# Attention rewritten for pairs of heads on two TensorE tiles

## The chip, the cores and the metric

The kernel runs on one core of one Trainium2 chip. A core has TensorE (PE; its weight loads are shown apart as PEld), VectorE (DVE), ScalarE (ACT), GpSimd (POOL) and the queues of SyncE (SP), all running on their own and meeting at semaphores. The metric is the device time of one execution in microseconds (us).

## The reference

Two stages follow one another. The attention has 4 batches of 8 heads, 768 positions of 64 numbers each. Keys are cut into 24 chunks of 32. For every query a bound per chunk is computed from the chunk's smallest and largest key; the six chunks with the highest bounds are kept, and the softmax runs over their keys up to the query's own position.

```
ub = sum(max(q * k_min, q * k_max))          # per query and chunk
top_chunks = argsort(where(causal, ub, -1e9))[-6:]
scores = q @ k.T / 8;  mask = (chunk in top_chunks) & (key <= query)
attn = softmax(where(mask, scores, -1e9));  out = attn @ v
```

The second stage is a mixture of experts over the 3072 rows of 512 numbers: each row goes to the expert with the highest gate logit (8 experts), each expert keeps its 80 rows with the highest gate weight, computes `gate * (relu(x @ w1) @ w2)`, and all other rows are zero.

## The kernel before

The attention phase runs through 32 heads one by one (L381 to L388), everything in float32. Per head:

- `prologue1` loads q, k and v and transposes q and k with TensorE (L267, L269), twelve transposes of 128 rows by 64 columns into psA and psB.
- `prologue2` copies them into `srhs` and `slhs` (ACT), makes the positive and negative part of q (`qstk`) and the chunk maxima and minima (`kstk`) on DVE, multiplies both (L282), takes the six best of 24 with six `max` instructions (L287), transposes the 0/1 selection (L292) and writes it, scaled to 0 or -80000, into rows 64 to 87 of `srhs` (L294). Rows 64 to 87 of `slhs` hold a fixed table of which key lies in which chunk. So the mask is part of the score matmul, which has 64 + 24 = 88 rows.
- `do_scores` computes the scores with keys on partitions, for each block of 128 keys only the queries from its own block on (L306; 768, 640, 512, 384, 256 and 128 columns). ACT takes the exponential (L311), DVE multiplies the diagonal block by a triangle (L314).
- `do_av` multiplies 21 blocks of the exponentials (as weights) by v with a column of ones (L323), so that column 64 of the result is the softmax sum; the queries lie on the output's partitions.
- `do_norm` divides on DVE and writes the rows in float32 and bf16 (L333 to L339). After a batch's last head it transposes the rows (L345), multiplies by the gate weights (L353) and computes gate weight and expert of each row (L360 to L375).

The second phase, behind a barrier (L390), sorts out the 80 rows per expert on DVE (L430 to L454), gathers them by a matmul with a 0/1 matrix (L480, L484), runs the experts (L497, L510), and scatters back in 24 turns: eight bf16 transposes (L516), a copy (L519), eight matmuls (L521), a copy and a store.

The order on each engine is the order in which the code issues. A helper class notes who wrote and read each buffer last and puts semaphore waits in front of an instruction. In the kernel before, an instruction also waits for an earlier one of its own engine when both write the same buffer, unless both are marked as accumulating; the transposes L267, L269, L292, L345 and L516 are not marked. There is one buffer of most kinds, so heads overlap only where the loop is written so: the transposes of the next head come before L323 of this one, and `prologue2` of the next head behind it.

Of the kernel before, what the change touches and what calls it, by code (L numbers as in the profile page):

```python
# [4 lines left out]
ALU = mybir.AluOpType  # L5
# [3 lines left out]
I32 = mybir.dt.int32  # L9
AX = mybir.AxisListType.X  # L10

NEGSEL = -1.0e9
BIGM = 8.0e4
CHUNK = 32
TOPK = 6
NCANDP = 16


class _Sync:
# [3 lines left out]
    def __init__(self, nc):  # L23
        self.nc = nc
        self.engines = {
            "pe": nc.tensor, "act": nc.scalar, "dve": nc.vector, "gp": nc.gpsimd,
            "sp": nc.sync, "acd": nc.scalar, "gpd": nc.gpsimd,
        }
        self.dma_engines = {"sp", "acd", "gpd"}
        self._cms = {}  # L30
        self.sems = {}
        self.cnt = {}
        self.last_write = {}
        self.last_reads = {}
        self.waited = {}
        for key in self.COMPUTE:
            self._mk(key)

    def _mk(self, key):
        cm = self.nc.semaphore("sy_" + key)  # L40
        self._cms[key] = cm
        self.sems[key] = cm.__enter__()
        self.cnt[key] = 0

    def sem(self, key):
        if key not in self.sems:
            self._mk(key)
        return self.sems[key]
# [5 lines left out]
    def _wait(self, waiter, semkey, val):  # L54
        if val <= 0:
            return
        wk = (waiter, semkey)
        if self.waited.get(wk, 0) >= val:
            return
        self.waited[wk] = val  # L60
        self.engines[waiter].wait_ge(self.sems[semkey], val)

    def op(self, ekey, fn, reads=(), writes=(), dsem=None, accum=False):
        is_dma = ekey in self.dma_engines
        semkey = dsem if dsem is not None else ekey
        inc = 16 if is_dma else 1
        for r in reads:
            w = self.last_write.get(r)
            if w is not None and not (accum and w[0] == semkey and w[2]):
                self._wait(ekey, w[0], w[1])  # L70
        for wres in writes:
            w = self.last_write.get(wres)
            if w is not None and not (accum and w[0] == semkey and w[2]):
                self._wait(ekey, w[0], w[1])
            for sk, sv in self.last_reads.get(wres, {}).items():
                self._wait(ekey, sk, sv)
        inst = fn()
        if semkey not in self.sems:
            self.sem(semkey)
        newval = self.cnt[semkey] + inc  # L80
        inst.then_inc(self.sems[semkey], inc)
        self.cnt[semkey] = newval
        for wres in writes:
            self.last_write[wres] = (semkey, newval, accum)
            self.last_reads[wres] = {}
        for r in reads:
            d = self.last_reads.setdefault(r, {})
            d[semkey] = max(d.get(semkey, 0), newval)
        return inst

    def wait_final(self, waiter, semkey):
        self._wait(waiter, semkey, self.cnt[semkey])

    def barrier_all(self):
        for wtr in self.COMPUTE:
            for prod in self.COMPUTE:
                if prod != wtr:
                    self._wait(wtr, prod, self.cnt[prod])


def bass_quest_chunk_select__then__topk_capacity_drop_kernel(
# [15 lines left out]
    NQT = S // 128  # L117
    NCH = S // CHUNK
    TOKT = B * NQT
    DB = Dm // 128  # L120
    FB = Fd // 128
    LROWS = D + NCH
    SCALE = 1.0 / float(D) ** 0.5
    EC = E * CAP
    assert S % 128 == 0 and D == 64 and Dm == H * D and CAP % 8 == 0 and E == 8
# [3 lines left out]

    with ExitStack() as pers, ExitStack() as phA, ExitStack() as phB:  # L130

        _alcnt = [0]

        def al(stack, shape, dt=F32, psum=False, nm=None):
            _alcnt[0] += 1
            name = (nm or "t") + "_" + str(_alcnt[0])
            if psum:
                return stack.enter_context(nc.psum_tensor(name, list(shape), dt))
            return stack.enter_context(nc.sbuf_tensor(name, list(shape), dt))

        x_bf = al(pers, [128, TOKT, Dm], BF16, nm="x_bf")
        gate_sb = al(pers, [128, TOKT], nm="gate_sb")
        eidx_sb = al(pers, [128, TOKT], nm="eidx_sb")
        ident_f = al(pers, [128, 128], nm="ident_f")
        ident_bf = al(pers, [128, 128], BF16, nm="ident_bf")
        caus_c = al(pers, [128, NQT, NCH], nm="caus_c")
        cbias_c = al(pers, [128, NQT, NCH], nm="cbias_c")
        ctri_c = al(pers, [128, 128], nm="ctri_c")
        esel_c = al(pers, [128, E, E], nm="esel_c")
        bmask_c = al(pers, [8, E, CAP], nm="bmask_c")  # L150
        wg_sb = al(pers, [128, DB, E], nm="wg_sb")
        ones8 = al(pers, [8, 128], nm="ones8")

        NSLOT = 4
        w1slot = [al(pers, [128, DB, Fd], BF16, nm="w1slot") for _ in range(NSLOT)]
        w2slot = [al(pers, [128, FB, Dm], BF16, nm="w2slot") for _ in range(NSLOT)]


        sy = _Sync(nc)

        with nc.Block() as blk:

            @blk.sync
            def _body(_unused):
# [5 lines left out]

                tmp_i = al(phA, [128, 1024], I32, nm="tmp_i")
                psA = al(phA, [128, 768], F32, True, nm="psA")
                psB = al(phA, [128, 768], F32, True, nm="psB")
# [389 lines left out]
```

## Time and profile before

| | us |
|---|---|
| runs of the kernel before | 1590.32, 1596.66, 1603.84 (median 1596.66) |
| span of the profiled execution | 1590.3 |
| its own time | the span; the fastest run shown, 1590.32, is the same within 0.1 |
| attention phase in the profile | 0 to 1112 |
| expert phase | 1112 to 1590 |
| TensorE busy | 1180.6 (74%) |
| VectorE busy | 604.3 (38%) |

The page shows the engines' busy time, then the chain that ended last, then groups of instructions by line. A group's row gives the tile written, the tiles read, the weights' shape (partitions * columns) and the moving operand's shape. A float32 matmul stands in the trace as two matmul records with a weight load each (L323 is 21 matmuls a head, 672 in all, and has 1344 records); a transpose and a bf16 matmul stand as one.

### The profile page before, as it was taken

Reading aid. Unit: us, or ns where it says so; the run is one execution under the profiler, and the core shown is the slowest. Engines: PE = TensorE matmul, PEld = TensorE weight load, DVE = VectorE, ACT = ScalarE, POOL = GpSimd, SP = SyncE. Lnnn points to the kernel's source line nnn. Section 1 sums busy time; section 2 is a strip of 40 time slices with the busy share of each in tenths; the row PEclk is TensorE's granted clock in tenths of the full one; section 3 lists DMA queues with packets and bytes.
Section 4 is the critical chain, followed back from the end, with each engine's and each line's share of the span. In section 5 each row is a group of like instructions: output and inputs, shape, how many; then the busy total and the mean of one; then the engine's idle time right before and its main releaser. Section 6 shows DMA issues by size and latency. Waiting matters only on the chain.

```text
span 1590.3 us, 11275 instructions
## 1 busy us (share of the span) xinstructions
PE 1180.6 (74%) x4100; PEld 691.1 (43%) x4100; DVE 604.3 (38%) x1812; ACT 193.6 (12%) x337; POOL 15.2 (1%) x26
## 2 busy tenths in 40 slices
PE   6888886888888678988967898885661004778887
PEld 3556554555655445645644565553110002433332
DVE  4343342344343243343314333432338995111010
ACT  1111111112112112112101111111000000010000
POOL 2000000000000000000000000000000000100000
PEclk9555555555555555555555555555785556875555
DMA  9401000001000000100100010000000000660101
GB/s 191 86 15 30 15 15 15 15 15 30 15 15 20 10 15 21 25 15 21 25 1 15 20 25 15 5 6 0 0 0 0 0 0 0 111 114 34 40 33 40
DMA packets 91846, 42.68 MB, mean 27 GB/s; under 512 B 76432, under 2 KB 84624, under 8 KB 91792
## 3 DMA queue, kind: packets, MB, share of 16 engines
q0 software_dynamic: 12544, 16.78, 6.1%
q1 hardware_dynamic: 54160, 18.90, 4.8%
q10 hardware_dynamic: 25088, 6.29, 1.8%
q8 instruction: 33, 0.54, 0.1%
q14 instruction: 21, 0.17, 0.0%
HBM read 52.45 MB, written 6.29 MB: 37 GB/s over the span
## 4 chain that ended last, share of the span: by engine, by line
PE 73%; DVE 21%; issue 3%; ACT 2%; DMA 1%; SPq 0%; DVEq 0%; POOL 0%; ACTq 0%; POOLq 0%
PE psE L323 16%; PE psA L306 11%; PE psB L306 8%; PE psX L521 5%; PE psB L292 5%; PE psC L282 4%; PE psT L516 4%; PE psG L435 3%; PE psB L269 3%; PE psA L345 3%; PE psA L267 3%; PE psC L353 3%; DVE top_37 L287 2%; DVE I_64 L446 2%; DVE V_63 L445 2%
## 5 line engine op out<-in xcount | busy, mean ns | idle before, releaser
L323 PE MATMUL psE<-v_ext,e_sb 128*128 128x65 f32 x1344 | 260.2, 384 | 0.0
L323 PEld LDWEIGHTS psE<-v_ext,e_sb 128*128 128x128 f32 x1344 | 259.1, 302 | 0.0
L306 PE MATMUL psA<-srhs,slhs 88*128 88x512 f32 (+1 forms) x256 | 201.1, 889 | 44.4 <-DVE srhs L294 30.2
L306 PE MATMUL psB<-srhs,slhs 88*128 88x128 f32 (+2 forms) x256 | 158.9, 724 | 1.8
L292 PE MATMUL psB<-ident_f,sel 128*24 128x128 f32 x192 | 74.5, 388 | 86.6 <-DVE sel L290 77.2
L311 ACT ACTIVATE e_sb<-psA 128x768 f32<-128x768 f32 (+2 forms) x96 | 57.3, 596 | 573.6 <-PE psA L306 573.6
L306 PEld LDWEIGHTS psA<-srhs,slhs 88*128 88x128 f32 x256 | 69.6, 317 | 125.0 <-PE psA L306 52.1
L306 PEld LDWEIGHTS psB<-srhs,slhs 88*128 88x128 f32 x256 | 73.9, 319 | 108.7 <-PE psB L306 52.2
L314 DVE TENSOR_TENSOR e_sb<-e_sb,ctri_c 128x128 f32<-128x128 f32 x192 | 55.9, 291 | 141.8 <-ACT e_sb L311 141.7
L521 PE MATMUL psX<-Ybf,selTj 80*128 80x512 bf16 x192 | 86.2, 630 | 18.8 <-DVE selTj L519 18.8
L285 DVE TENSOR_TENSOR ubm<-psC,cbias_c 128x144 f32<-128x144 f32 x32 | 9.9, 308 | 201.7 <-PE psC L282 201.7
L435 PE MATMUL psG<-rhsX,esel_c 128*8 128x512 f32 x96 | 55.5, 741 | 39.5 <-DVE rhsX L430 24.6
L267 PE MATMUL psA<-ident_f,q_nat 128*64 128x128 f32 x192 | 80.0, 417 | 4.4 <-DMA q_nat<-in_q_dram 4.4
L269 PE MATMUL psB<-ident_f,k_nat 128*64 128x128 f32 x192 | 80.0, 417 | 3.1 <-DMA k_nat<-in_k_dram 0.5
L462 PE MATMUL psG<-bd_67,ones_12 8*128 8x512 f32 (+1 forms) x4 | 2.5, 776 | 104.6 <-DVE bd_67 L456 104.6
L282 PE MATMUL psC<-kstk,qstk 128*128 128x24 f32 x384 | 76.5, 355 | 4.5 <-DVE kstk L279 4.5
L292 PEld LDWEIGHTS psB<-ident_f,sel 128*24 128x24 f32 x192 | 18.2, 95 | 137.2 <-DVE sel L290 80.9
L282 PEld LDWEIGHTS psC<-kstk,qstk 128*128 128x128 f32 x384 | 75.6, 298 | 4.8 <-DVE kstk L279 4.8
L345 PE MATMUL psA<-ident_f,x_f_46 128*128 128x128 f32 x96 | 45.3, 472 | 38.8 <-DVE x_f_46 L336 22.3
L519 DVE COPY selTj<-psT 80x1024 bf16<-80x1024 bf16 x24 | 16.5, 686 | 151.1 <-PE psT L516 151.1
L516 PE MATMUL psT<-ident_bf,sel_all 128*80 128x128 bf16 x192 | 62.1, 324 | 9.7
L294 DVE TENSOR_SCALAR srhs<-psB 24x768 f32<-24x768 f32 x32 | 30.4, 949 | 86.9 <-PE psB L292 86.9
(93 smaller groups left out, 1008.8 us busy)
## 6 DMA issues: line engine op xcount, KB each, us to landing
w1slot<-in_moe_w_dram POOLq DMA_DIRECT2D x8, 1024.0 KB, 18.0
w2slot<-in_moe_w_dram POOLq DMA_DIRECT2D x8, 1024.0 KB, 18.5
q_nat<-in_q_dram SPq DMA_DIRECT2D x32, 192.0 KB, 2.8
k_nat<-in_k_dram SPq DMA_DIRECT2D x32, 192.0 KB, 3.1
v_ext<-in_v_dram ACTq DMA_DIRECT2D x32, 192.0 KB, 2.6
out_dram<-otile SPq DMA_DIRECT2D x24, 256.0 KB, 2.0
wg_sb<-in_moe_w_gate_dram SPq DMA_DIRECT2D x1, 16.0 KB, 1.9
```

What stands on the lines that cost most here:

```text
L267: sy.op("pe", lambda qt=qt, buf=buf: pe.transpose(psA[0:D, ts(qt)], q_nat[buf][:, qt, :], ident_f[:]), reads=[f"qnat{buf}", "ident_f"], wr ...
L269: sy.op("pe", lambda qt=qt, buf=buf: pe.transpose(psB[0:D, ts(qt)], k_nat[buf][:, qt, :], ident_f[:]), reads=[f"knat{buf}", "ident_f"], wr ...
L282: sy.op("pe", lambda o_ap=o_ap, qt=qt: pe.matmul(o_ap, qstk[:, ts(qt)], kstk[:], start=True, stop=True), reads=["qstk", "kstk"], writes=[" ...
L292: sy.op("pe", lambda qt=qt: pe.transpose(psB[0:NCH, ts(qt)], sel[:, qt, :], ident_f[:]), reads=["sel", "ident_f"], writes=["psB"])
L306: sy.op("pe", lambda sps=sps, c0=c0, c1=c1, lhsK=lhsK, kt=kt: pe.matmul(sps[:, c0:c1], lhsK, srhs[:, 128 * kt + c0:128 * kt + c1], start=T ...
L311: sy.op("act", lambda sps=sps, kt=kt, ncol=ncol: ac.activation(e_sb[kt][:, 0:ncol], sps[:, 0:ncol], ACTF.Exp, scale=SCALE), reads=[pskey], ...
L314: sy.op("dve", lambda kt=kt: ve.tensor_tensor(e_sb[kt][:, 0:128], e_sb[kt][:, 0:128], ctri_c[:], ALU.mult), reads=[ekey, "ctri_c"], writes ...
L323: sy.op("pe", lambda lhsA=lhsA, kt=kt, qb=qb, buf=buf: pe.matmul(o_of(qb), lhsA, v_ext[buf][:, kt, :], start=(kt == 0), stop=(kt == qb)), ...
L345: sy.op("pe", lambda bd=bd, qt=qt: pe.transpose(psA[:, ts(qt)], x_f32[:, qt, bd * 128:(bd + 1) * 128], ident_f[:]), reads=["x_f32", "ident ...
L435: sy.op("pe", lambda e=e, c0=c0, c1=c1, rx=rx: pe.matmul(psG[0:8, c0:c1], esel_c[:, e, :], rx[:, c0:c1], start=(e == 0), stop=(e == E - 1) ...
L516: sy.op("pe", lambda j=j, e=e: pe.transpose(psT[0:CAP, ts(e)], sel_all[:, j, e * CAP:(e + 1) * CAP], ident_bf[:]), reads=["sel_all", "iden ...
L521: sy.op("pe", lambda e=e: pe.matmul(psX[:, 0:Dm], selTj[:, ts(e)], Ybf[:, e, :], start=(e == 0), stop=(e == E - 1)), reads=["selTj", "Ybf" ...
```

## The change

The attention is written anew for pairs of heads (16 pairs), and the helper class too. The expert phase's instructions are the same. In parts:

- Two heads lie side by side on partitions: head 0 on 0 to 63, head 1 on 64 to 127. One 128 by 128 transpose (L354) serves both.
- The bounds use one block-diagonal table for both heads and two accumulating matmuls per block of queries (L375, L377), `q * k_min + relu(q) * (k_max - k_min)`; the first block of 128 queries is left out, since it has no more than four chunks.
- The scores (L405) have 64 rows, and the two heads alternate between the upper and the lower half of TensorE's rows, with outputs in two PSUM banks. The mask is a separate bf16 matmul of 64 rows per head added to them (L411): -65536 for chunks that are not selected, transposed in bf16 (L392).
- The exponential of both heads is one ACT instruction of up to 1024 columns (L416). The triangle is set on GpSimd by `affine_select` (L420). GpSimd also adds up the exponentials over key blocks (L436).
- The values (L447) have v as weights (64 columns), so that the two heads lie on the output's lower and upper partitions, each with half of TensorE's columns. The softmax sums come from matmuls with one column of ones (L458). One matmul per block of 128 queries (L469) turns the result back into rows and gives the gate logits as well; DVE divides (L476, L480). `gate` works on 6 blocks at once.
- The loop is pipelined over pairs: bounds of pair i+1 stand between scores and values of pair i, transposes of pair i+2 behind the values. q, k and v are loaded three pairs ahead. The weights of the first four experts are loaded one half each behind the first eight pairs.
- The new helper class makes TensorE wait for no write or read of its own, and other engines only for their own writes; waits that another wait implies are left out.

```diff
-                for gidx in range(NG):
-                    do_scores(gidx)
-                    if gidx + 1 < NG:
-                        prologue1(gidx + 1)
-                    do_av(gidx)
-                    if gidx + 1 < NG:
-                        prologue2(gidx + 1)
-                    do_norm(gidx)
...
+        for res in r:
+            for sk, val in self.lw.get(res, {}).items():
+                want((sk, val), ekey == "pe")
+        for res in w:
+            for sk, val in self.lw.get(res, {}).items():
+                want((sk, val), ekey == "pe")
+            for sk, val in self.lr.get(res, {}).items():
+                want((sk, val), not is_dma)
...
+    STEPS = [
+        [(0, 0, 512, 0)],
+        [(1, 128, 640, 0)],
+        [(2, 256, 768, 0)],
+        [(0, 512, 768, 0), (4, 512, 768, 256)],
+        [(3, 384, 768, 0), (1, 640, 768, 384)],
+        [(5, 640, 768, 0)],
+    ]
...
+                    for st, pieces in enumerate(STEPS):
+                        s = st % 2
+                        for pi, (kt, q0, q1, c) in enumerate(pieces):
+                            for h in range(2):
+                                pr = slice(h * 64, h * 64 + 64)
+                                o = SC[s][:, h * 512 + c:h * 512 + c + q1 - q0]
+                                op("pe", lambda: pe.matmul(o, kT[j][pr, ts(kt)], qT[j][pr, q0:q1], start=True, stop=False),
...
+                            for h in range(2):
...
+                                op("pe", lambda: pe.matmul(o, ind[pr, ts(kt)], unsT[j][pr, b0 - 128:q1 - 128],
...
+                        op("act", lambda: ac.activation(Ex[st][:], src, ACTF.Exp, scale=SCALE),
...
+                        op("gp", lambda: gp.affine_select(a, a, pattern=[[0, 2], [1, 128]], compare_op=ALU.is_ge, fill=0.0,
...
+                            op("gp", lambda: gp.tensor_tensor(o, in0, in1, ALU.add),
...
+                            for h in range(2):
...
+                                op("pe", lambda: pe.matmul(OB[pr, q0:q1], vn[s][:, kt, h, :], Ex[st][:, h, c:c + q1 - q0],
...
+                            a = Ex[0][:, h, 0:128] if t == 0 else ES[:, h, ts(t)]
+                            op("pe", lambda: pe.matmul(o, a, one1[:], start=True, stop=True),
...
+                            op("pe", lambda: pe.matmul(OB[:, bk * 512 + m * XW:bk * 512 + (m + 1) * XW], oT[:, ts(t)], xr[:, p, :],
...
+                for i in range(NP):
+                    scores(i)
+                    if i + 1 < NP:
+                        bounds(i + 1)
+                    values(i)
+                    if i + 3 < NP:
+                        load(i + 3)
+                    if i + 1 < NP:
+                        unselT(i + 1)
+                    if i + 2 < NP:
+                        transposes(i + 2)
+                    if i < 2 * NSLOT:
+                        wload(i // 2, i % 2)
+                    sums(i)
+                    rows(i)
+                    if i % NPB == NPB - 1:
+                        gate(i // NPB)
```

TensorE, before, one head (the transposes of the next head stand ahead of the values L323; L306 are the scores):

```order
L267 MATMUL psA<-ident_f,q_nat 64x128
L269 MATMUL psB<-ident_f,k_nat 64x128
L323 MATMUL psE<-v_ext,e_sb 128x65 x21
L282 MATMUL psC<-kstk,qstk 128x24 x6
L292 MATMUL psB<-ident_f,sel 24x128 x6
L306 MATMUL psA<-srhs,slhs 128x512
L306 MATMUL psA<-srhs,slhs 128x256
```

Between the values L323 and the next scores L306 stand the bounds and the mask of the very head whose scores follow.

TensorE, in the change, one pair from its third score step on (L405 scores, L411 mask, L375 and L377 bounds of the next pair, L447 values, L392 and L354 transposes for later pairs, L458 sums, L469 rows; `x2` are the two heads):

```order
L405 MATMUL SC_17<-qT,kT 128x512 x2
L411 MATMUL SC_17<-unsT,ind 128x512 x2
...
L375 MATMUL M_20<-kbd,qT 128x48
L377 MATMUL M_20<-kbd,rq 128x48
...
L447 MATMUL OB<-Ex,vn 64x512 x2
L447 MATMUL OB<-Ex,vn 64x384 x2
...
L392 MATMUL MB<-ident_bf,uns 128x128 x5
L354 MATMUL SC_17<-ident_f,qn 128x128 x6
L354 MATMUL SC_18<-ident_f,kn 128x128 x6
L458 MATMUL M_20<-one_63,Ex 128x1 x2
L458 MATMUL M_20<-one_63,ES 128x1 x10
L469 MATMUL OB<-xr,oT 128x144 x6
```

Every heavy float32 matmul now stands next to one of the other head, and between scores and values, where the head before had the chain L282 to L294, the bounds of another pair stand.

GpSimd, in the change, one pair but for its last addition (Ex are the exponentials, ES their sums; sy_act and sy_gp are semaphores of ScalarE and of GpSimd itself):

```order
L420 AFFINE_SELECT Ex<-Ex 128x2x128 [waits sy_act] x2
L436 TENSOR_TENSOR ES<-Ex 128x2x384 [waits sy_gp]
L420 AFFINE_SELECT Ex<-Ex 128x2x128 [waits sy_act]
L436 TENSOR_TENSOR ES<-ES,Ex 128x2x256 [waits sy_gp]
L420 AFFINE_SELECT Ex<-Ex 128x2x128 [waits sy_act]
L436 TENSOR_TENSOR ES<-Ex 128x2x256 [waits sy_gp]
L436 TENSOR_TENSOR ES<-ES,Ex 128x2x128 [waits sy_gp]
L436 TENSOR_TENSOR ES<-ES,Ex 128x2x256 [waits sy_gp]
L420 AFFINE_SELECT Ex<-Ex 128x2x128 [waits sy_act]
L436 TENSOR_TENSOR ES<-ES,Ex 128x2x128 [waits sy_gp]
L436 TENSOR_TENSOR ES<-ES,Ex 128x2x384 [waits sy_gp]
L420 AFFINE_SELECT Ex<-Ex 128x256 [waits sy_act]
```

Before, GpSimd had no instruction between the heads; now six selects and eight additions per pair stand in one queue, and the values on TensorE read what the selects write.

## Rows read from the trace of the kernel before

**Rows 1.** The page: its first line, the engines' busy time, the chain by engine.

```profile
span 1590.3 us, 11275 instructions
PE 1180.6 (74%) x4100; PEld 691.1 (43%) x4100; DVE 604.3 (38%) x1812; ACT 193.6 (12%) x337; POOL 15.2 (1%) x26
...
PE 73%; DVE 21%; issue 3%; ACT 2%; DMA 1%; SPq 0%; DVEq 0%; POOL 0%; ACTq 0%; POOLq 0%
```

**Rows 2.** Windows: stretch, its length, busy by engine, granted TensorE clock, DMA.

```profile
0.00:1112.00 1112.00, 914.62 (x3104) 592.97 (x3104) 417.88 (x1647) 172.28 (x297) 8.45 (x17) 0.54 0.12 25
...
1197.00:1302.00 105.00, 0.44 (x1) 0.44 (x2) 103.33 (x55) 0.00 (x0) 0.00 (x0) 0.51 0.00 0
...
1415.00:1590.00 175.00, 143.75 (x386) 52.72 (x384) 17.15 (x25) 14.33 (x24) 0.00 (x0) 0.51 0.10 36
```

**Rows 3.** Timeline of TensorE, one head: start, length, line, operands, count, [idle before].

```profile
631.90 0.39 PE L267 MATMUL psA<-ident_f,q_nat 128*64 128x128 f32 x1
...
634.97 9.08 PE L323 MATMUL psE<-v_ext,e_sb 128*128 128x65 f32 x42
643.84 2.70 PE L282 MATMUL psC<-kstk,qstk 128*128 128x24 f32 x12
648.95 2.62 PE L292 MATMUL psB<-ident_f,sel 128*24 128x128 f32 x6 [2.41 <-DVE sel L290]
652.61 3.35 PE L306 MATMUL psA<-srhs,slhs 88*128 88x512 f32 x4 [1.04 <-DVE srhs L294]
...
660.03 1.49 PE L306 MATMUL psB<-srhs,slhs 88*128 88x384 f32 x2
661.30 1.06 PE L306 MATMUL psA<-srhs,slhs 88*128 88x256 f32 x2
...
662.93 0.39 PE L267 MATMUL psA<-ident_f,q_nat 128*64 128x128 f32 x1
```

**Rows 4.** Groups by line and shape: busy time, mean ns, idle before.

```profile
L484 PE MATMUL psG<-sel_all,x_bf 128*128 128x128 bf16 x96 | 21.8, 227 | 0.0
```

**Rows 5.** Windows inside single stages, columns as in the second group.

```profile
622.00:632.00 10.00, 9.88 (x17) 4.07 (x16) 5.27 (x27) 3.03 (x6) 0.00 (x0) 0.50 0.00 1
635.00:643.80 8.80, 8.80 (x43) 8.80 (x43) 3.00 (x4) 1.44 (x2) 0.00 (x0) 0.50 0.21 47
1117.00:1121.00 4.00, 4.00 (x6) 0.58 (x5) 0.18 (x1) 0.00 (x0) 0.00 (x0) 0.50 0.00 0
1122.00:1124.00 2.00, 2.00 (x6) 0.36 (x4) 0.00 (x0) 0.00 (x0) 0.00 (x0) 1.00 0.00 0
...
579.00:583.00 4.00, 4.00 (x38) 4.00 (x38) 2.88 (x4) 0.55 (x1) 0.00 (x0) 1.00 0.44 100
```

**Rows 6.** Groups by line and shape, ScalarE.

```profile
L311 ACT ACTIVATE e_sb<-psA 128x768 f32<-128x768 f32 x32 | 25.9, 809 | 528.1 <-PE psA L306 528.1
...
L311 ACT ACTIVATE e_sb<-psB 128x128 f32<-128x128 f32 x32 | 8.9, 277 | 6.5 <-PE psB L306 6.5
```

**Rows 7.** Groups by line, GpSimd.

```profile
L235 POOL IOTA tmp_i<- 88x768 int32 x1 | 0.8, 764 | 0.6 <-DVE v_ext L232 0.6
L191 POOL IOTA tmp_i<- 128x144 int32 x1 | 0.3, 262 | 0.5 <-DVE ident_bf L188 0.5
```

**Rows 8.** Timeline of TensorE, one turn of the last loop.

```profile
1421.63 3.02 PE L516 MATMUL psT<-ident_bf,sel_all 128*80 128x128 bf16 x8
1425.43 3.60 PE L521 MATMUL psX<-Ybf,selTj 80*128 80x512 bf16 x8 [0.78 <-DVE selTj L519]
1428.82 0.31 PE L516 MATMUL psT<-ident_bf,sel_all 128*80 128x128 bf16 x1
```

**Rows 9.** Timeline, the end of the attention phase.

```profile
1070.28 0.16 DVE L333 TENSOR_SCALAR rec<-psE 128x1 f32<-128x1 f32 x1 [8.26 <-PE psE L323]
...
1111.91 0.15 DVE L375 CAST eidx_sb<-idx_52 128x1 f32<-128x1 uint32 x1
```

**Rows 10.** Timeline of TensorE, the first scores of the run.

```profile
21.43 3.36 PE L306 MATMUL psA<-srhs,slhs 88*128 88x512 f32 x4 [1.04 <-DVE srhs L294]
```

More of the change, by code (lines that the diff above doesn't have):

```diff
@@ L91, in wait_final, with _learn @@
-    def wait_final(self, waiter, semkey):
-        self._wait(waiter, semkey, self.cnt[semkey])
+    def _learn(self, clock, ev):
+        sk, val = ev
+        if clock.get(sk, 0) < val:
+            clock[sk] = val
+        best = None
+        for v, snap in reversed(self.snaps[sk]):
+            if v <= val:
+                best = snap
+                break
+        if best:
+            for k2, v2 in best.items():
+                if clock.get(k2, 0) < v2:
+                    clock[k2] = v2
@@ L94, in barrier_all, with _implied, wait_for @@
+    def _implied(self, a, b):
+        c = {}
+        self._learn(c, a)
+        return c.get(b[0], 0) >= b[1]
+    def wait_for(self, waiter, keys):
+        for k in keys:
+            if self.cnt.get(k, 0):
+                self.queue[waiter].wait_ge(self.sems[k], self.cnt[k])
+                self._learn(self.clock.setdefault(self.stream.get(waiter, waiter), {}), (k, self.cnt[k]))
     def barrier_all(self):
@@ new lines, in _body @@
+                load(0)
+                v128 = iv(128, [1, 128])
+                op("gp", lambda: gp.iota(v128, pattern=[[-1, 128]], base=0, channel_multiplier=1), w=["ti"])
+                op("dve", lambda: ve.tensor_scalar(ident_f[:], v128, 0, None, ALU.is_equal), r=["ti"], w=["ident_f"])
+                for j in range(2):
+                    op("dve", lambda: ve.memset(kbd[j][:], 0.0), w=KBD[j])
+                op("dve", lambda: ve.memset(uns[:], 0.0), w=["uns"])
+                op("dve", lambda: ve.memset(one1[:], 1.0), w=["one1"])
@@ new lines, in _body @@
+                transposes(0)
+                bounds(0)
+                unselT(0)
+                transposes(1)
+                for i in range(NP):
[15 more added lines that the diff above has]
+                        gate(i // NPB)
@@ L390, in _body @@
                 sy.barrier_all()
+                XB = [f"x_bf{i}{bk}" for i in range(NP) for bk in range(2)]
+                XS = [f"xb{j}" for j in range(TOKT)]
+                EI = [f"eidx{b}" for b in range(B)]
+                GS = [f"gate{b}" for b in range(B)]
                 phA.close()
-                psG = al(phB, [128, TOKT * 128], F32, True, nm="psG")
-                psX = al(phB, [128, 512], F32, True, nm="psX")
-                psT = al(phB, [128, 1024], BF16, True, nm="psT")
```

736 lines of the change are left out of this document (387 added, 349 removed), and 3 rows, old and new, of the table AVS.

## Prediction

> **What bounds the kernel now.** I read the page first: TensorE is busy for 74% of the span and for 73% of the chain [rows 1]. The windows by stage then split the span [rows 2]: attention ends at 1112.0, the experts take the other 478.3 (1590.3 - 1112.0), 105 of them on DVE alone. The timeline of one head [rows 3] shows where attention's time lies: from transpose to transpose a head takes 31.0 us (631.90 to 662.93), of which TensorE waits 2.41 and 1.04 for DVE and otherwise works. [...]
>
> **Unit prices, at 0.50.** A float32 matmul is two records. L306 with 384 columns takes 661.30 - 660.03 = 1.27 us [rows 3], 3.31 ns per column. L323 has only 65 columns, yet 42 records take 643.84 - 634.97 = 8.87 [rows 3], 0.42 us per matmul; its weight loads fill the same stretch, as the third number of that window says [rows 5], so 0.42 us is what a float32 matmul with 128 weight columns costs however narrow it is. At clock 1.00, 38 records in 4 us [rows 5] make it 0.21. A transposed float32 block costs (634.97 - 631.90) / 12 = 0.26. [...]
>
> **The change, per pair of heads.** What TensorE issues, at 0.50:
> - 12 transposes x 0.26, taken as before although they load 128 columns instead of 64 and no longer wait on each other: 3.1.
> - Bounds, 10 matmuls x 0.42: 4.2. Mask transposes, 5 x 128 bf16 columns: 0.5.
> - Scores: 2688 columns per head, 8.9 us, and 2560 mask columns, 2.1; for two heads 22.0 one after the other, 11.0 if the halves of the array work fully side by side.
> - Values: 2688 columns per head, 8.9; 17.8 or 8.9.
> - Sums, 12 x 0.42: 5.0. Rows, 6 x 144 columns: 2.9.
>
> No row here has two matmuls in different halves of the array, so the overlap is the first unknown, between none and full. I take overlap, but by the order in which matmuls come: TensorE takes them in program order [rows 3], so head 1's first record can start only once head 0's second has started. With N the time of one bf16 pass, a piece is 2N alone, 2N shared by the heads, then head 1's second record beside head 0's mask (2N): 6N against 5N full and 10N serial. Scores then cost 13.4; values, without a mask, reach 4N per pair of matmuls, 8.9. Sum: 3.1 + 4.2 + 0.5 + 13.4 + 8.9 + 5.0 + 2.9 = 38.0 at 0.50 and 19.0 at 1.00, against 62 for two heads before.
>
> [...]
>
> **The clock** is the second unknown. L306, 88 rows, stays at 0.50 through 10 us without a gap; L323 stays there too in this head; L435, 128 rows and 512 columns, is at 0.50 for its first 4 us and at 1.00 afterwards; L323 holds 1.00 in a head that enters it so [rows 5]. In the change rows, scores and values use all 128 rows, if the halves overlap, and follow each other with only the bounds between; the sums, one column wide, are the weak place. So I take 4 us at 0.50 from the start of the rows stage (2.9 of rows, 1.1 of scores), the other 12.3 of scores at 1.00 as 6.2, bounds 2.1, values 4.5, transposes 1.8, and for the sums 3.8, midway between 2.5 and 5.0.
>
> **GpSimd** is the third. Its only compute rows are index patterns: (764 - 262) ns over 768 - 144 elements is 0.80 ns per element plus 0.15 us [rows 7]. A pair has six selects of 256 elements and eight additions of 3840 in all. Bounds: 0.80 throughout gives 6.4 us per pair (5376 x 0.80 + 14 x 0.15), three streams for two reads and a write, 2.4, gives 15. I take 2.4 for additions and 0.8 for selects, 12.5, since an addition moves three times the data of a pattern. [...] At 12.5 GpSimd stays below TensorE's time, but its queue is serial: the last select stands behind seven additions. An exponential of 1024 columns costs 1.02 us (809 ns at 768 and 277 ns at 128 [rows 6], so 0.83 per column), so from the first exponential to the last select some 14 us pass, and values that could start at 9 us and end at 14 end at about 17: a stall of 3. Behind each of the first eight pairs GpSimd also issues one weight load; TensorE reads it only in the expert phase, so I cost it at nothing.
>
> A pair: 4 + 6.2 + 2.1 + 4.5 + 3 + 1.8 + 3.8 = 25.4, with 0.6 for seven changes of stage 26. ACT has 5.5 us of exponentials and 3.3 of copies by the same line, DVE 25 instructions at its mean of 0.33 us (604.3 / 1812 [rows 1]), 8.3; both lie beside TensorE's work, and without that cover either would bound a pair at under 10.
>
> **Around the pairs.** The first scores start at 21.4 now [rows 10]; more loads, constants and the bounds of a whole pair make it 25. The last pair has no bounds and transposes, -5. The end of attention takes 41.6 now (1070.3 to 1111.9 [rows 9]), since the last head's division, four rounds of transposes and copies, the gate matmuls and six chains of small instructions follow one another; afterwards the division of the last pair and one such chain remain, some 13 instructions x 0.33 = 4. Attention: 25 + 16 x 26 - 5 + 4 = 440.
>
> **Experts.** A turn of the last loop takes 1428.82 - 1421.63 = 7.19; eight transposes and the copy take 3.80 of it (1421.63 to 1425.43), since each waits for the one before it [rows 8]. Unchained they stream at 0.11 each: 8 x 0.11 + 0.22 + 0.80 for the copy = 1.90. That is 1.9 x 24 = 46 saved, with the clock left at 0.51 [rows 2]. Multiplying the rows by their gate loses its chain too, 2. 478.3 - 48 = 430.
>
> **Sum:** 440 + 430 = 870. The profiled execution is the span, 1590.3, and the median of the runs is 0.4% above it, which I neglect.
>
> **Rivals.**
> - *The clock does not rise in the scores.* For: L306 never got it. Against: it had 88 rows. Values then begin at 0.50 (4 + 2.5): 2.9 + 13.4 + 4.2 + 6.5 + 1.8 + 3.8 + 0.6 = 33.2, 985 in all; never anywhere, 39 a pair, 1078. Chance 0.27.
> - *The halves do not overlap.* For: nothing here shows overlap in float32. Against: rows and PSUM banks are disjoint. Scores 22.0 at 0.50, values 4 + 6.9: 46 a pair, about 1190; 30 a pair if all of it ran at 1.00 (930), 56 if none (1350). Chance 0.17.
> - *Slower than before: GpSimd becomes the bound.* Its queue is serial and feeds the values. Against: it decides only from (1590.3 - 430 - 24) / 16 = 71 us per pair, which means 10 us per select instead of 0.35, or additions five times my upper bound. Price then 1600 and more. For: no select has a row. Chance 0.02.
> - *The change does not do what it says* would leave 1112 + 430 = 1542: only if every pair still took two heads' time. Chance 0.01.
>
> My forecast, with the pair at 21 (fast GpSimd, all at 1.00) to 29, is 780 to 920 and has 0.53. The range to 1150 takes in the slow clock and the mildest part of serial halves; it starts at 770.
>
> **Numbers.** 870, 770 to 1150. One per cent either way, 16 us, is what this kernel's runs can tell. Only the GpSimd rival is slower; a result within 1% needs the sum to be off by 700 us. Faster 0.96, same 0.01, slower 0.03.
>
> **What would show it.** Right: for each piece of L405 the second head's records start while the first head's run; the granted clock of attention above 0.75; TensorE idle before the last L447 matmuls, released by GpSimd L420; L516's eight transposes in about 1.1 us. [...]

## The result and the profile after

The changed kernel takes 761.7 us (median; 759.5 to 796.7 in four runs) against 1597.7 for the kernel before: a ratio of 0.476 [0.473, 0.479]. That is faster, as forecast, and 8 us below the low end of the range. Ratios compare the executions within 1.5% of each kernel's fastest, while medians and ranges take all. The rows are from another execution of the changed kernel, with a span of 760.3; the longest took 796.7, and nearly all of the difference between the two lies in the last loop (below).

The page: span, busy time, granted clock in 40 slices.

```profile
span 760.3 us, 8659 instructions
PE 511.2 (67%) x3632; PEld 312.4 (41%) x3636; DVE 318.3 (42%) x619; ACT 159.4 (21%) x221; POOL 209.9 (28%) x254
...
PEclk9999999999999999999868887555555699969999
```

Windows: attention and the last loop (answering to [rows 2]).

```profile
0.00:382.00 382.00, 338.95 (x2640) 238.08 (x2640) 134.58 (x453) 138.12 (x181) 203.18 (x245) 0.95 0.40 73
...
682.00:758.00 76.00, 55.86 (x376) 29.91 (x376) 15.81 (x23) 14.33 (x24) 0.00 (x0) 1.00 0.21 80
```

Attention ends at 382 where it was 1112, with TensorE's clock at 0.95 where it was 0.54. The last loop takes some 76 us at 1.00 where 175 were at 0.51. In the clock row the nines up to the middle are attention, the low stretch behind them the sorting, and the end the last loop. From the end of attention to the last loop it is 298 us (382 to 680), 303 before (1112 to 1415).

One pair on TensorE (answering to the head of [rows 3]):

```profile
178.89 1.13 PE L405 MATMUL SC<-qT,kT 64*128 64x512 f32 x4
...
180.02 1.02 PE L405 MATMUL SC<-qT,kT 64*128 64x512 f32 x4
...
185.43 0.42 PE L375 MATMUL M<-kbd,qT 128*128 128x48 f32 x2
...
187.79 2.15 PE L447 MATMUL OB<-Ex,vn 128*64 128x512 f32 x12
190.86 2.60 PE L447 MATMUL OB<-Ex,vn 128*64 128x128 f32 x28 [0.91 <-POOL Ex L420]
193.91 0.44 PE L447 MATMUL OB<-Ex,vn 128*64 128x128 f32 x4 [0.46 <-POOL Ex L420]
194.29 0.45 PE L392 MATMUL MB<-ident_bf,uns 128*128 128x128 bf16 x5
...
195.89 0.50 PE L458 MATMUL M<-one,Ex 128*128 128x1 f32 x4
...
198.49 1.90 PE L469 MATMUL OB<-xr,oT 128*128 128x144 f32 x12
200.32 2.08 PE L405 MATMUL SC<-qT,kT 64*128 64x512 f32 x4
```

From scores to scores this is 21.4 us: scores 6.5, bounds 2.4, values 6.5 with two waits for GpSimd's selects in them (0.91 and 0.46), transposes 1.6, sums 2.6, rows 1.8. The next pair begins with the same four score records in 2.08 us instead of 1.13; the windows inside the pairs show why.

```profile
179.00:199.00 20.00, 18.51 (x157) 12.77 (x158) 6.63 (x20) 8.51 (x11) 12.87 (x15) 1.00 0.53 97
200.00:203.00 3.00, 3.00 (x10) 1.36 (x11) 2.48 (x9) 0.44 (x2) 0.00 (x0) 0.50 1.19 190
```

Nine such dips, of some 3.5 us each, lie in the 16 pairs, and a tenth begins at 374 and runs on past the end of attention. All ten begin in the sums or in the rows behind them: this one at 199.9, with the sums from 195.89 and the rows from 198.49. The mean pair is (382 - 25) / 16 = 22.3 us. A turn of the last loop (answering to [rows 8]) now is 686.83 - 683.69 = 3.14 us:

```profile
683.69 0.61 PE L652 MATMUL psT<-ident_bf,sel_all 128*80 128x128 bf16 x8
685.09 1.90 PE L657 MATMUL psX<-Ybf,selTj 80*128 80x512 bf16 x8 [0.78 <-DVE selTj L655]
686.83 0.61 PE L652 MATMUL psT<-ident_bf,sel_all 128*80 128x128 bf16 x8
```

### The profile page after: what moved, and what is told of

Read it like the earlier page. It is cut to its first block, busy times and chain, and to the rows that moved or that the text cites. A ratio compares the mean times of both kernels' runs of the same rounds, so it can differ in the third digit from the quotient of the medians.

```text
span 794.8 us, 8663 instructions
## 1 busy us (share of the span) xinstructions
PE 546.3 (69%) x3636; PEld 325.8 (41%) x3636; DVE 318.5 (40%) x619; ACT 159.5 (20%) x221; POOL 209.9 (26%) x254
## 4 chain that ended last, share of the span: by engine, by line
PE 43%; DVE 25%; POOL 22%; DMA 4%; ACT 3%; issue 2%; DVEq 0%; POOLq 0%; ACTq 0%
POOL ES L436 18%; PE psX L657 9%; PE psG L570 7%; PE M L458 5%; DVE I L581 4%; PE SC L405 4%; DVE V L580 4%; POOL Ex L420 4%; PE OB L469 4%; DVE Gc L583 4%; DMA w2slot<-in_moe_w_dram 3%; DVE rhsX L565 3%; PE psG L615 3%; PE SC L354 2%; ACT Ex L416 2%
## 5 line engine op out<-in xcount | busy, mean ns | idle before, releaser
L405 PE MATMUL SC<-qT,kT 64*128 64x512 f32 (+3 forms) x512 | 104.2, 495 | 4.5 <-ACT Ex L416 2.5
L436 POOL TENSOR_TENSOR ES<-ES,Ex 128x512 f32<-128x512 f32 (+1 forms) x96 | 104.4, 1087 | 7.8
L416 ACT ACTIVATE Ex<-SC 128x1024 f32<-128x1024 f32 x96 | 86.0, 915 | 84.9 <-PE SC L411 83.3
L447 PE MATMUL OB<-Ex,vn 128*64 128x256 f32 (+3 forms) x704 | 84.5, 382 | 23.6 <-POOL Ex L420 23.6
L657 PE MATMUL psX<-Ybf,selTj 80*128 80x512 bf16 x192 | 71.0, 536 | 20.2 <-DVE selTj L655 18.1
L420 POOL TENSOR_SCALAR_AFFINE_SELECT Ex<-Ex 128x256 f32<-128x256 f32 x96 | 41.5, 433 | 156.7 <-ACT Ex L416 156.7
L447 PEld LDWEIGHTS OB<-Ex,vn 128*64 128x64 f32 x704 | 44.1, 139 | 61.1 <-POOL Ex L420 37.7
L405 PEld LDWEIGHTS SC<-qT,kT 64*128 64x128 f32 x512 | 43.1, 197 | 45.5 <-ACT Ex L416 28.3
L436 POOL TENSOR_TENSOR ES<-Ex 128x768 f32<-128x768 f32 (+1 forms) x32 | 49.2, 1538 | 2.7
L615 PE MATMUL psG<-sel_all,x_bf 128*128 128x512 bf16 x96 | 29.2, 406 | 27.5 <-DVE x_bf L610 24.8
L565 DVE TENSOR_TENSOR rhsX<-gval,ident_f 128x3072 f32<-128x3072 f32 x8 | 26.9, 3358 | 46.3 <-PE psG L570 46.2
```

The costliest lines, as they stand in the source:

```text
L405: op("pe", lambda: pe.matmul(o, kT[j][pr, ts(kt)], qT[j][pr, q0:q1], start=True, stop=False), r=[f"kT{j}", f"qT{j}"], w=[f"SC{s}"], inc=False)
L416: op("act", lambda: ac.activation(Ex[st][:], src, ACTF.Exp, scale=SCALE), r=[f"SC{s}"], w=[f"E{st}"])
L420: op("gp", lambda: gp.affine_select(a, a, pattern=[[0, 2], [1, 128]], compare_op=ALU.is_ge, fill=0.0, base=0, channel_multiplier=-1), r=[f ...
L436: op("gp", lambda: gp.tensor_tensor(o, in0, in1, ALU.add), r=[f"E{s2}", f"E{st}", "E0"] + [f"ES{t}" for t in range(q0 // 128, q1 // 128)], ...
L447: op("pe", lambda: pe.matmul(OB[pr, q0:q1], vn[s][:, kt, h, :], Ex[st][:, h, c:c + q1 - q0], start=(n == 0), stop=last), r=[f"vn{s}{h}", f ...
L565: op("dve", lambda gvb=gvb, identb=identb: ve.tensor_tensor(rhsX[:], gvb, identb, ALU.mult), r=["gval", "ident_f"], w=["rhsX"])
```

## The experiments

Two sums had to be explained: attention 58 us shorter than forecast (382 for 440), and the expert phase 52 shorter (378 for 430). Each time below stands beside runs of the kernel before in the same session, at 1592 to 1598 us; the attention phase is also compared by where it ends in the profile, since it doesn't vary with the last loop.

### The changed kernel again

> The changed kernel unaltered, to have a profile of an execution at the usual time (the profiled one took 796.7 us, the three others 759.5 to 761.7). Theory 1 (the last loop of the expert phase runs at granted clock 1.00 when nothing breaks it): attention ends at about 384 us as in the profile at hand, and all 24 turns of the last loop take 3.2 us, 77 us in all instead of 115. Rival (the difference lies in attention): attention ends near 350 and the last loop again takes 115.

756.1 to 792.4 us in four runs, ratio 0.475 [0.471, 0.479]. In the execution of 762 us the last loop is at 1.00 from its first turn to its end; attention ends at 382.1, and at 384.1 in the one of 796.7. In that one too the loop comes to 1.00 in its first turn, until a copy waits for the output tile's store (its timeline, then the window behind the wait):

```profile
712.27 0.61 PE L652 MATMUL psT<-ident_bf,sel_all 128*80 128x128 bf16 x8
...
714.24 0.60 ACT L660 ACTIVATE otile<-psX 128x512 f32<-128x512 f32 x1 [4.31 <-DMA out_dram<-otile]
...
714.98 3.56 PE L657 MATMUL psX<-Ybf,selTj 80*128 80x512 bf16 x8 [2.10 <-ACT otile L660]
...
718.34 1.06 PE L652 MATMUL psT<-ident_bf,sel_all 128*80 128x128 bf16 x8
```

```profile
714.00:794.00 80.00, 65.83 (x232) 29.78 (x232) 9.62 (x14) 9.55 (x16) 0.00 (x0) 0.51 0.14 53
```

The same eight transposes take 0.61 us before the wait and 1.06 behind it, and the clock doesn't come back in 80 us, with TensorE busy for 82% of them. But the execution of 762 us has such a wait as well, some 25 us later in its loop, and keeps its clock (the transposes behind it take 0.61):

```profile
736.52 1.89 PE L657 MATMUL psX<-Ybf,selTj 80*128 80x512 bf16 x8 [2.03 <-ACT otile L660]
```

So one late store can go with the loss of the clock and need not. Without the self-waits and with one output tile, the loop reached 1.00 in eight of the profiles of this case. Each of the eight has one such wait, of 1.37 to 2.41 us; six lost the clock right behind it, and two, with 2.03 and 2.32 us, didn't.

### The self-waits put back

```diff
                     for e in range(E):
+                        pe.wait_ge(sy.sems["pe"], sy.cnt["pe"])
                         op("pe", lambda j=j, e=e: pe.transpose(
```

> In the last loop of the expert phase each transpose waits for TensorE's own instruction before it, as in the kernel before; nothing else changed. Theory (the waits cost themselves and the clock): 24 turns from 3.2 to 7.2 us, the clock at 0.50, +95 us, about 855. Rival (the prediction's sum: the waits alone, 1.9 us a turn): +46 us, about 806, with the clock left where it was.

863.6 us, ratio 0.540 [0.538, 0.543], attention ending at 380.8: 102 us more than the changed kernel, in the last loop. The timeline shows a turn of 7.46 us, with the eight matmuls behind the transposes at 3.59, about the 3.60 of [rows 8]:

```profile
700.02 3.04 PE L653 MATMUL psT<-ident_bf,sel_all 128*80 128x128 bf16 x8
703.83 3.59 PE L658 MATMUL psX<-Ybf,selTj 80*128 80x512 bf16 x8 [0.78 <-DVE selTj L656]
707.48 3.04 PE L653 MATMUL psT<-ident_bf,sel_all 128*80 128x128 bf16 x8
```

The granted clock is up for part of the first turn and 0.50 from 684 to the end, without a late store. At the half level a turn without the waits takes 5.23 us (next experiment), at the full one 3.14. So the waits cost 2.2 us per turn themselves and 2.1 by the clock. The theory holds, in this kernel.

### The same edit in the kernel before

```diff
-                            reads=["sel_all", "ident_bf"], writes=["psT"])
+                            reads=["sel_all", "ident_bf"], writes=["psT"], accum=True)
```

> The kernel before, with one thing of the change in it: the eight transposes of the selection matrix in each turn of the last loop are issued without a wait of TensorE for its own transpose before. Theory 1 (the clock): with the waits gone the granted clock leaves its half level in the last loop, as it does in the changed kernel, and a turn falls from 7.19 us to about 3.2; 24 turns give back about 95 us, so about 1500 us, and the granted clock between 1415 us and the end is 0.9 or more. Rival (the waits alone, as predicted): the clock stays at 0.51, 24 x 1.9 = 46 us come back, about 1550 us.

1523 to 1546 us, median 1539.9, ratio 0.963 [0.958, 0.969]. Here the rival was right for the profiled execution (1545 us), in which the whole loop is at the half level, with turns of 1435.16 - 1429.93 = 5.23; the quickest, 1523, has no profile.

```profile
1414.00:1541.00 127.00, 107.20 (x386) 49.06 (x384) 17.17 (x25) 14.33 (x24) 0.00 (x0) 0.50 0.13 48
```

```profile
1429.93 1.06 PE L516 MATMUL psT<-ident_bf,sel_all 128*80 128x128 bf16 x8
...
1435.16 1.06 PE L516 MATMUL psT<-ident_bf,sel_all 128*80 128x128 bf16 x8
```

The loop has the same instructions as that of the changed kernel. Both enter it at the half level, behind w2 matmuls that waited for their weights (2.35 us here and 3.75 in the changed kernel, with eight matmuls in 3.60 and 3.61 us behind the waits); the changed kernel's execution rose to 1.00 and this one didn't, though no store is late in it. So taking the waits away makes the full clock possible, not certain.

### What decides the level: a longer entry, more output tiles

On top of that edit, the eight transposes of the first turn issued five times over:

```diff
-                    for e in range(E):
+                    for e in list(range(E)) * (5 if j == 0 else 1):
```

> The kernel before without the self-waits of its last loop's transposes, and with the eight transposes of the first turn issued five times over, 32 more of about 0.13 us each at the half level, so that TensorE works some 9 us on end where the loop begins. Theory (the loop holds whichever level it enters with): the clock rises at the entry and the turns of 3.2 us hold it: 24 x (5.3 - 3.2) = 50 us less than the version without the 32, about 1495 us, with a granted clock of 1.00 in most of the last loop. Rival (the loop as it stands in the kernel before pulls the clock back to the half level, whatever it enters with): 1540 us plus 4, no turn at 1.00 after the first few.

1531 to 1553 us, median 1539.1, ratio 0.962 [0.954, 0.971]: no gain in the time. The timeline shows both expectations to be half right:

```profile
1432.24 0.61 PE L516 MATMUL psT<-ident_bf,sel_all 128*80 128x128 bf16 x8
...
1433.48 0.60 ACT L524 ACTIVATE otile<-psX 128x512 f32<-128x512 f32 x1 [3.58 <-DMA out_dram<-otile]
...
1434.22 2.01 PE L521 MATMUL psX<-Ybf,selTj 80*128 80x512 bf16 x8 [1.37 <-ACT otile L524]
...
1436.03 1.06 PE L516 MATMUL psT<-ident_bf,sel_all 128*80 128x128 bf16 x8
```

The clock rose at the entry and some three turns ran at 1.00. Then a late store made TensorE wait 1.37 us instead of 0.78, and from there on the loop stayed at 0.50. Next, four output tiles with a semaphore each, without the self-waits, once with the long entry and once with the usual one:

```diff
-                    sy.op("act", lambda: ac.activation(otile[:], psX[:, 0:Dm], ACTF.Copy), reads=["psX"], writes=["otile"])
-                    sy.op("sp", lambda j=j: sp.dma_start(out[ts(j), :], otile[:]), reads=["otile"], writes=[f"out{j}"], dsem="d_out")
...
+                    sy.op("act", lambda j=j: ac.activation(otile[j % 4][:], psX[:, 0:Dm], ACTF.Copy), reads=["psX"], writes=[f"otile{j % 4}"])
+                    sy.op("sp", lambda j=j: sp.dma_start(out[ts(j), :], otile[j % 4][:]), reads=[f"otile{j % 4}"], writes=[f"out{j}"], dsem=f"d_out{j % 4}")
```

> The kernel before without the self-waits, with the 32 further transposes at the entry and with four output tiles in the last loop. Theory (the loop holds the level it has; a stall such as the 1.37 us for a late store in the version with one tile is what takes it to the half level): the clock rises at the entry and stays at 1.00 to the end, 24 turns of about 3.15 us, 1490 to 1500 us, with executions within 12 us of each other. Rival (the loop falls back by itself in some turns): 1520 to 1545 us.

> The kernel before without the self-waits and with four output tiles, without the long entry. Theory: the level is decided where the loop is entered, and there the eight w2 matmuls run at the half level behind their transfer; with the usual entry the clock does not rise, turns of 5.25 us, 1535 to 1546 us, as with one tile. Rival (with the late stores gone the loop rises by itself): under 1510 us.

With both: 1495.7, 1506.5, 1506.9 and 1508.9 us, three of them above the 1490 to 1500 that I expected, ratio 0.939 [0.933, 0.945]. Without the long entry: 1494.2, 1494.2, 1499.8 and 1545.1, ratio 0.934 [0.927, 0.940]. Windows of the last loop, of the one and of the other:

```profile
1428.00:1504.00 76.00, 57.15 (x397) 31.03 (x394) 16.48 (x24) 13.79 (x24) 0.00 (x0) 1.00 0.22 80
```

```profile
1420.00:1495.00 75.00, 55.93 (x376) 29.93 (x376) 16.68 (x25) 13.83 (x24) 0.00 (x0) 1.00 0.22 81
```

My theory for the second of them was wrong: by the times, the loop rose with the usual entry in three executions of four, and the fourth, at 1545, has the time of a loop at the half level throughout. What the profiles show is that the loop without the self-waits and without a late store kept one level from its second turn on: 76 and 75 us at 1.00 in these two, 127 us at 0.50 in the execution of 1545 with one tile. No store is late with four tiles: the 24 turns take some 75 to 76 us. The long entry left no execution low in four, which is too few to call its use shown.

### Values: one head behind the other

```diff
-  for n, (kt, q0, q1, st, c) in enumerate(lst):
-      for h in range(2):
+  for h in range(2):
+      for n, (kt, q0, q1, st, c) in enumerate(lst):
```

> In the values, all pieces of head 0 first, then all of head 1, so that neighbours in program order use the same half of TensorE's columns. Theory (the two halves overlap): the L447 stage grows from 2 x 2.2 us of streaming to about twice that, 4 us more per pair, of which 1 lies in the present waits for GpSimd: 16 x 3 to 4.5 = 50 to 70 us slower, about 820. Rival (halves do not overlap, the gain came from elsewhere): no change, within 8 us.

799.4 to 836.7 us, ratio 0.500 [0.497, 0.504]; attention ends at 423.3, 41 later: 2.6 us per pair, less than expected. The values of a pair take 2.15 + 5.95 = 8.1 us of work, with clock 0.96 over the attention:

```profile
203.48 2.15 PE L447 MATMUL OB<-Ex,vn 128*64 128x512 f32 x6
206.56 5.95 PE L447 MATMUL OB<-Ex,vn 128*64 128x128 f32 x38 [0.93 <-POOL Ex L420]
```

```profile
0.00:423.00 423.00, 387.13 (x2640) 269.80 (x2640) 134.02 (x452) 138.39 (x181) 202.95 (x245) 0.96 0.37 65
```

With the heads taken in turns they are 4.76 (next experiment). The halves of the columns do work side by side; of the 3.3 us some went into the waits for GpSimd, of which only the first is left.

### GpSimd: selects of steps 4 and 5 ahead of the additions of steps 3 and 4

```diff
+                    late = []
...
+                        late.append(st)
+                        if st in (3, 4):
+                            continue
-                        for (s2, c2, q0, q1) in ADDS:
+                        for st, (s2, c2, q0, q1) in [(x, y) for x in late for y in ADDS]:
...
+                        late = []
```

> On GpSimd, the selects of score steps 4 and 5 ahead of the additions of steps 3 and 4. Theory (values wait for selects that stand behind additions): the two idle stretches ahead of L447 (0.91 and 0.46 us per pair released by L420) go, the additions end when they did: 16 x 1.0 to 1.4 = 16 to 22 us faster, about 740. Rival (the queue's end decides, since the sums need the last addition): the wait moves to L458 and the time stays within 5 us.

733.6 to 763.0 us, ratio 0.462 [0.458, 0.466], attention ending at 363.3: 19 us less, as expected. The 44 value matmuls of a pair run without a gap:

```profile
180.98 4.76 PE L452 MATMUL OB<-Ex,vn 128*64 128x512 f32 x44
```

The windows of 335 us of attention, of the changed kernel and of this one, show one thing more: TensorE has less idle time, and a lower clock.

```profile
25.00:360.00 335.00, 310.36 (x2467) 216.59 (x2469) 118.59 (x399) 127.02 (x167) 187.17 (x219) 0.95 0.38 70
```

```profile
25.00:360.00 335.00, 330.68 (x2583) 240.03 (x2579) 109.96 (x403) 132.41 (x174) 196.57 (x232) 0.91 0.38 70
```

So the dips inside the pairs don't come from the waits for GpSimd: without them some 60 of these 335 us are at the half level, (1 - 0.91) x 2 x 335, instead of some 33. Here too every fall, 14 in all, comes in the sums or the rows.

### Scores: both heads on the upper half

```diff
-                                pr = slice(h * 64, h * 64 + 64)
+                                pr = slice(0, 64)
...
-                                   r=[f"ind{h}", f"unsT{j}"], w=[f"SC{s}"], inc=last)
+                                   r=["ind0", f"unsT{j}"], w=[f"SC{s}"], inc=last)
```

> The changed kernel with the scores and mask matmuls of both heads on the upper 64 rows of the array, so that both heads take head 0's operands; it leaves out head 1's scores. The instructions, their number and order stay. Theory (the two halves' score matmuls overlap, as the values' do): a score step of 512 columns goes from 1.28 us to 2.1 us or more, 4 to 5.5 us per pair, 65 to 90 us in all; the attention ends at 445 to 475 us in place of 382, about 825 to 850 us in all, and with twice the time for the same columns the clock stays where it was. Rival 1 (the scores are paced by the exponentials, the halves do little there): under 1.5 us per pair, below 790 us. Rival 2 (it is work on both halves at once that lifts TensorE's clock): the clock goes to 0.50 in the scores, 12 us or more per pair, over 950 us.

The first of these edits stands in the scores and again in the mask. 913 to 960 us, median 938.5; in the profiled execution (935) attention ends at about 524 (the next phase's first matmul is at 528.6 instead of 387.0, 142 later). Timeline, then windows:

```profile
203.50 1.88 PE L405 MATMUL SC<-qT,kT 64*128 64x512 f32 x4
205.22 0.59 PE L411 MATMUL SC<-unsT,ind 64*128 64x512 bf16 x2
205.65 1.88 PE L405 MATMUL SC<-qT,kT 64*128 64x512 f32 x4
```

```profile
137.00:166.00 29.00, 29.00 (x76) 17.06 (x76) 4.50 (x21) 5.75 (x7) 12.68 (x15) 0.50 0.31 57
168.00:248.00 80.00, 80.00 (x570) 58.49 (x566) 26.39 (x78) 28.65 (x38) 38.62 (x45) 1.00 0.49 87
...
25.00:520.00 495.00, 495.00 (x2588) 333.10 (x2587) 119.39 (x403) 134.04 (x174) 198.58 (x232) 0.80 0.27 47
```

A step of 512 columns takes 205.65 - 203.50 = 2.15 us, against 1.30 with two halves (180.02 to 181.32), a wait for ScalarE included: the overlap of the scores is shown. At clock 1.00 a pair is 24.4 us from scores to scores, 3 more than in the profile above and less than I expected, 48 in all. Of the other 94 the clock explains some 82 by the windows, (1 - 0.80) x 495 - (1 - 0.95) x 335. TensorE is busy in every microsecond of the 495, and yet stands at 0.50 for stretches of 29 us and more. Eight of its ten falls come in the sums or the rows, as in the changed kernel; but after six of these it came back only in the values of the next pair, 27 to 34 us later, where in the changed kernel it came back after some 3.5. Rival 2 was partly right, but it isn't the rule that one half means half a clock: the same work stood at 1.00 for 80 us.

### No mask matmul, and no pipelining over pairs

The mask matmuls (L411) taken out, and the order of the loop over pairs:

```diff
-                transposes(0)
-                bounds(0)
-                unselT(0)
-                transposes(1)
                 for i in range(NP):
+                    transposes(i)
+                    bounds(i)
+                    unselT(i)
                     scores(i)
-                    if i + 1 < NP:
-                        bounds(i + 1)
                     values(i)
...
-                    if i + 1 < NP:
-                        unselT(i + 1)
-                    if i + 2 < NP:
-                        transposes(i + 2)
```

> The changed kernel without the chunk-mask matmuls into the scores; it leaves out the chunk mask, so all chunks up to the diagonal are attended to. Theory: a score step is paced by two things that lie within a tenth of each other, the exponential (1.02 us for 2 x 512 columns, with its wait about 1.2) and TensorE's 1.28, and the values wait for GpSimd in any case; so the mask matmuls cost less than 0.5 us per pair on the path: 745 to 762 us. Rival (TensorE's order of six paces the scores, and four is what is left): 5 steps give back up to 0.43 us each, 2 us per pair, about 725 us. A third case: less work for TensorE lets its clock fall more often, slower than 765 us.

> The changed kernel with the pairs one after the other: transposes, bounds, unselected rows, scores and values of a pair are issued before those of the next; the tile halves, the mask matmul and the last loop stay. Theory (pipelining carries a large part): in each pair the waits for the two bound matmuls, VectorE's top-chunk work of some 5 us, the transposes' copies and the last selects of GpSimd stand uncovered, 8 to 11 us per pair, 130 to 175 us, and TensorE's clock falls to its half level in those gaps, which adds 1 to 3 us per pair: 890 to 990 us. Rival (the halves and the clock give nearly all, pipelining little): under 3 us per pair, 760 to 810 us.

Without the mask: 758.6 to 793.4 us, and attention ends 3.8 us earlier (the next phase's first matmul at 383.2 instead of 387.0), 0.24 per pair. That is no clear gain, since three profiles of one and the same attention end at 380.8, 382.1 and 384.1. As expected, the exponentials (1.02 us each) keep the pace.

Without pipelining: 995.9 us, ratio 0.620 [0.619, 0.622]; attention ends near 593 (first matmul behind it at 597.6), 13 us per pair later, near the upper end of what I expected. The timeline shows the waits that stood covered, 3.16 + 3.69 + 1.93 = 8.8 us against 1.4; the rest I put down to the clock, which is 0.75 over the attention.

```profile
216.00 4.50 PE L447 MATMUL OB<-Ex,vn 128*64 128x128 f32 x32 [3.16 <-POOL Ex L420]
...
231.51 0.63 PE L375 MATMUL M<-kbd,qT 128*128 128x48 f32 x2 [3.69 <-DVE kbd L368]
...
237.91 0.71 PE L392 MATMUL MB<-ident_bf,uns 128*128 128x128 bf16 x5 [1.93 <-DVE uns L386]
```

### Selects ahead and four output tiles together

> The version with the selects of steps 4 and 5 ahead of GpSimd's additions, and four output tiles with a semaphore each in the last loop in place of one, so that a late store holds up no copy. Theory (the clock is lost in the last loop in those executions in which a store is late): the quick executions stay as they were with the selects ahead, 733 to 745 us, and the spread of that version (733 to 763 us) closes to under 10 us. Rival (the late store is not what loses the clock): the spread stays at about 30 us with four tiles. A smaller gain of up to 5 us may come where a turn waits for the store in any execution.

730.1 to 738.6 us, median 735.1, ratio 0.461 [0.459, 0.464]. The spread of 29 us with one tile closes to 8.5, and this is the best version measured by its median: by the ratios (0.4758 - 0.4613) x 1592 = 23 us under the changed kernel. Its quick executions are no quicker than with one tile (0.462); what is gone is the long ones.

## Why the prediction was right and where it was wrong

**Right: the halves overlap. Wrong: the pattern named.** A step of 512 columns is 2.15 us on one half at clock 1.00. N, the time of a mask of 512 columns, is 0.215 us there (two take 205.65 - 205.22 = 0.43), and a float32 record of 512 columns takes 2N (four take 205.22 - 203.50 = 1.72): 10N in all, the prediction's figure for halves in series. On two halves the prediction had head 1 start behind head 0's first record, 6N in all. The sign that was asked for, the second head's records beside the first's, is there, and more: the four records of a step start two by two, where on one half each starts 0.43 us behind the one before. Both of the first two start at 180.0 (first row, of the window 180.1 to 180.2), and the mask follows at 180.88, 4N later. That is full overlap. With 1N for both masks (0.21 us, 182.29 to 182.50) TensorE needs 5N = 1.08 us; that the step took 1.30, close to 6N = 1.29, comes from the wait of the next weights for ScalarE's exponential (second row):

```profile
L405 PE MATMUL SC<-qT,kT x2: 589/589/589, 180.0 to 180.0; 64*128 64x512 f32 x2
...
181.32 0.30 PEld L405 LDWEIGHTS SC<-qT,kT 64*128 64x128 f32 x4 [0.78 <-ACT Ex L416]
```

That the scores came to 6.5 us for the 6.2 forecast is luck: the overlap was taken too small, and the exponentials, which the prediction let run beside TensorE's work at no cost, hold TensorE up. Values came to 4.76 for 4.5. For the bf16 prices in its sum (2560 mask columns at 2.1 us, a transpose of the last loop at 0.11 with 0.22 more behind eight, about the mean of [rows 4]) the prediction shows no measurement. By them two masks of 512 columns take 2.1 x 1024 / 2560 / 2 = 0.42 us at 1.00, and eight transposes 8 x 0.11 + 0.22 = 1.10 at 0.50; the runs have 0.43 and 1.06.

**Right: GpSimd.** 12.5 us per pair were estimated; the groups give (41.5 + 40.6 + 34.8 + 29.0 + 28.9 + 20.2) / 16 = 12.2, the selects a little more than estimated and the additions a little less:

```profile
L420 POOL TENSOR_SCALAR_AFFINE_SELECT Ex<-Ex 128x256 f32<-128x256 f32 x96 | 41.5, 432 | 155.0 <-ACT Ex L416 155.0
L436 POOL TENSOR_TENSOR ES<-ES,Ex 128x512 f32<-128x512 f32 x32 | 40.6, 1268 | 2.6
L436 POOL TENSOR_TENSOR ES<-ES,Ex 128x256 f32<-128x256 f32 x48 | 34.8, 725 | 3.9
L436 POOL TENSOR_TENSOR ES<-ES,Ex 128x768 f32<-128x768 f32 x16 | 29.0, 1814 | 1.3
L436 POOL TENSOR_TENSOR ES<-Ex 128x768 f32<-128x768 f32 x16 | 28.9, 1809 | 1.3
L436 POOL TENSOR_TENSOR ES<-Ex 128x512 f32<-128x512 f32 x16 | 20.2, 1265 | 1.3
```

An addition costs (1814 - 725) / 512 = 2.1 ns per element and 0.18 us, where 2.4 and 0.15 were taken.

**Wrong by 58 us: the pair of 26.** In the prediction's frame it is (382 - 25 + 5 - 4) / 16 = 22.4. No single term carries that; nearly all were taken too long.
- Sums: 3.8, "midway" between the two levels, against 2.6 at the full clock, -1.2. They were called the weak place of the clock. They run at the full level in nearly every pair, yet all ten falls come in them or in the rows behind them: the place was right, and most of what it costs lies behind the sums.
- Values and stall: 4.5 + 3 against 6.5, -1.0. The last select ends 13.6 us after the first exponential starts (180.25 to 193.86), as estimated. But only 4 of the 44 records, 0.44 us, stand behind it, and the waits are 0.91 + 0.46.
- Rows and scores: 2.9 + 1.1 + 6.2 against 1.8 + 6.5 + 1.1, -0.8. The "4 us at 0.50" from the start of the rows are dips of some 3.5 us in ten pairs of 16 and not in each, which cost half their length, 10 x 1.75 / 16 = 1.1 per pair.
- Changes of stage: 0.6, for which the prediction had no row, against nothing seen.

**Wrong by about 50 us: "with the clock left at 0.51" in the last loop.** The eight transposes stream as forecast (1.06 us at the half level, 0.61 at the full one), and the 46 us for the waits alone are what the kernel before gave back in its execution of 1545. But without the waits the loop can hold 1.00, and then a turn is 3.14 instead of 5.23: 24 x 2.1 = 50 more. The forecast took the level of the kernel before as a property of the stage, though the waits that were removed had helped to set it. The waits for a late store, at which some executions lose the clock, also make the spread of 36 us between executions, which the prediction did not have.

**The rivals.** The clock does rise in the scores (1.00 from 179 to 199), the halves overlap (1.30 us a step, against 2.15 on one half), and GpSimd is no bound (busy for 203 of 382 us). Nor does the trace show time for the prediction's changes of stage: from values to transposes the next record starts as the last ends (194.29, against 193.91 + 0.44).

## What to carry to other kernels

When a change takes waits out of a TensorE stage that stands at the half clock, price the stage at both levels: here the waits were 46 us, and the clock that they had held down 50. A stage that can lose its level at one late store is worth more output buffers (four here), since that took away the long executions (730.1 to 738.6 us, where one tile gave 733.6 to 763.0). On an engine that takes its queue in order, as GpSimd did here, and feeds the critical path, put the short instructions that are waited for (the selects) ahead of the long ones that aren't (the additions): that was 19 us for a change of order.

## What the runs showed that I had not expected

- Unbroken work didn't secure TensorE's full clock. With the scores on one half it was busy for 29.00 of 29.00 us at 0.50, and 80.00 of 80.00 at 1.00.
- With the values' heads one behind the other, all 128 rows in use, the attention kept 0.96; with the scores' heads one behind the other on 64 rows it had 0.80. Whether it is the rows that matter wasn't tried by itself, and why the clock falls behind the sums in ten pairs of the changed kernel and not in the other six stays open.
- Removing idle time lowered the mean clock, 0.95 to 0.91, and still gave 19 us.
